# Attention in pairs of score tiles, with the weight conversion regrouped around it

## The chip, the cores and the metric

The kernel runs on one NeuronCore of a Trainium2 chip. Five engines have instruction queues of their own: TensorE (PE; its weight loads are shown apart as PEld), VectorE (DVE), ScalarE (ACT), GpSimd (POOL) and SyncE (SP), which here issues every DMA. The metric is the device time of one execution in microseconds (us).

## The reference

Two stages, in float32. Attention: batch 4, 8 heads, 576 positions, head width 64.

```
scores = q @ k.T / 8 + bias          # bias[h,i,j] = MLP(log1p|i-j| / log1p(max(i,1)))
attn   = softmax(scores); x = attn @ v
```

Then a mixer on x (4 x 576 x 512), with weights handed over as 64-bit floats:

```
u   = x + (x.T @ U @ V).T            # U 576x32, V 32x576
out = u + max(u @ w_ch1, 0) @ w_ch2  # 512 -> 2048 -> 512
```

## The kernel before, in words

**Order of the work.** The bias table of all heads is made first (about the first 60 us): a loop of 38 rounds, in each one score-bias block that PE multiplies, ACT copies out and SP stores to `bias_dram`. Then attention runs over 16 pairs of heads (batch 4 x 4 pairs), and then the mixer MLP. Nothing reorders the instructions: the schedule is manual, so each engine runs its instructions in the order in which the Python code emits them, and a waiting instruction holds all that stand behind it on its engine.

**A pair.** The 2 x 576 query rows of a pair are cut into 9 score tiles of 128 rows, s = 0 to 8 (tile 0 holds the last 64 rows of both heads). `slot(p, s)` (L489) emits the work of one tile:

- `scores` (L292): PE multiplies into a PSUM buffer `sc` (two of them, pool `psS`; tile 0 takes 8 matmuls, the others 4), and DVE adds the bias and takes the row extreme (L319). A buffer is free for the tile after next when DVE has read it.
- `exps` (L335): ACT takes the exponential in place (L338); for s = 0, 4, 8 it also sums up (L343).
- `tr`, `tr_m`, `tr_mid` (L378, L388, L397): PE transposes earlier tiles 128 x 128 at a time into one of three PSUM banks, and DVE or ACT copies them into `pt`. The first tile of a block is copied by DVE, the second by ACT; the last block of a pair is copied by ACT, and is transposed in slots 0 and 1 of the next pair.
- `av` (L411): the product of `pt` with v, in two halves of the query rows (half 0 is 320 columns wide, half 1 256). A half has five steps j. Steps 0 to 3 use 64-column weights, one per head, so that the two heads fill the two halves of the array; step 4 takes both heads in one 128-column matmul (L429). Each float32 matmul of these shows as two PE instructions. `AV_NEW` and `AV_OLD` say in which slot which steps stand: half 0 of a pair in its own slot 8 (j = 0, 1) and in slot 2 of the next pair (j = 2 to 4), half 1 in slots 4 (j = 0 to 2) and 6 (j = 3, 4) of the next pair. So a pair has four groups of products.
- `assemble` (L434): the product, copied by ACT to `ot`, is transposed again and scaled by DVE into `x_sb`.
- `recip` (L345): the reciprocal of the row sums on DVE, and for tile 0 a scaled copy `pm` on POOL (L358), which `tr_m` transposes in slot 5.

**Preparation of q and k.** `load_pair` brings the q and k of a pair into `raw` (one buffer), and `prep_ops` (L141) splits it on POOL into `hi` and `lo` by four instructions: `hi` (L153), its low part (L159), `hi`, `lo`. The scores of the next pair need all four. For pair 1 the raw data comes in three pieces (`second`, L692), of which the last, 16 KB, is issued in round 34 of the bias loop.

**Conversion.** The 64-bit weights are turned to float32 in jobs of 256 columns (`conv_ops`, L173): a load, then size and low (ACT, L185 and L188), clamp, shift, join (DVE, L191, L197, L203), add (POOL, L208), and a finish. `pipeline` (L618) cuts the jobs into three groups each, `[size, low, clamp]`, `[shift]`, `[join, add]`, and `background` emits the next groups behind the slots that `conv_at` names (six groups a pair). The first job is U (160 columns), three are V, whose finish `fin_v` is a copy on ACT and a subtraction on DVE (L611), and 16 are weights. Two empty groups stand behind the first loads.

**Mixer inside attention.** After each batch `mix_t` and five `mix_h` make u from x; they stand in pairs 5, 9 and 13 (`mix_t` ahead of slot 0) and, for the last batch, in the MLP.

Of the kernel before, what the change touches and what calls it, by code (L numbers as in the profile page):

```python
# [25 lines left out]
P = 128  # L26
# [11 lines left out]
AV_NEW = {8: (0, 1)}  # L38
AV_OLD = {2: [(0, 2), (0, 3), (0, 4)], 4: [(1, 0), (1, 1), (1, 2)], 6: [(1, 3), (1, 4)]}
# [5 lines left out]
def kernel(  # L45
# [365 lines left out]
    def av(p, hf, j):  # L411
        d = pair[p]
        pt = d["pt", hf]
        n = 320 if hf == 0 else 256
        v = v_t[p]
        if j == 0:
            d["o", hf] = psA.tile([P, 512], F32, tag="a", name="o")
        o = d["o", hf]
        if j < 4:
            for hd in range(2):  # L420
                mm(  # L421
                    o[hd * D : (hd + 1) * D, 0:n],
                    lhsT=v[:, (4 * hd + j) * D : (4 * hd + j + 1) * D],
                    rhs=pt[:, 5 * hd + j, :],
                    start=(j == 0),
                    stop=False,
                )
        else:
            mm(o[:, 0:n], lhsT=v[:, 8 * D : 8 * D + P], rhs=pt[:, 4, :], start=False, stop=True)  # L429
            ot = otp.tile([P, 320], F32, tag="ot", name="ot")  # L430
            copy("a", ot[:, 0:n], o[:, 0:n])
            d["ot", hf] = ot
# [56 lines left out]
    def slot(p, s):  # L489

        new, old = p < NP, p > 0
        if new:
            scores(p, s)
        if old and s == 0:
            tr(p - 1, 3, 0, "a")
        elif old and s == 1:
            tr(p - 1, 3, 1, "a")
            tr_mid(p - 1, 1, "d")
        elif old and s == 4:
            assemble(p - 1, 0)  # L500
# [11 lines left out]
        if s > 0 and new:
            recip(p, s - 1)
        elif s == 0 and old:
            recip(p - 1, 8)
        if old:
            for hf, j in AV_OLD.get(s, ()):
                av(p - 1, hf, j)
        if new:
            for j in AV_NEW.get(s, ()):  # L520
                av(p, 0, j)
# [96 lines left out]
    def pipeline(jobs):  # L618
# [5 lines left out]
        for i, (_, o, fin) in enumerate(ops):  # L624
# [3 lines left out]
            groups += [[size, low, clamp], [shift], [join, add]]  # L628
# [40 lines left out]
    for i in range(len(order) + 2):  # L669
# [18 lines left out]
        if i in (13, 17, 34):  # L688
# [7 lines left out]
    loads += [o for c in (4, 0, 1) for o in bias_loads(c, 1)] + [lambda: load_pair(2)]  # L696
    loads += [o for c in (2, 3) for o in bias_loads(c, 1)]
# [32 lines left out]
    for p in range(NP):  # L730
        if p > 0:
            new_pair(p)
        if 0 < p < HP - 1:
            bias[p + 1] = big.tile([P, 9 * S], F32, tag=f"big{p + 1}", name=f"bias{p + 1}")
            loads = [o for c in (4, 0, 1, 2, 3) for o in bias_loads(c, p + 1)]
        for s in range(9):
            if s == (1 if p else 0) and p < NP - 1:
                prep = prep_ops(p + 1)
            if s in ((2, 3, 4, 5) if p else (0, 1, 2, 3)) and p < NP - 1:
                prep.pop(0)()  # L740
            if s == 7 and 0 < p < NP - 2:
                load_pair(p + 2)
            if s == 7 and p + 1 < NP:
                load_v(p + 1)
            for o in loads[0:2]:
                o()
            del loads[0:2]
            if p > 0 or s not in early.values():
                if p > HP and p % HP == 1 and s == 0:
                    mix_t(p // HP - 1)  # L750
                slot(p, s)
                background(conv_at.get(s, 0))
            if p > HP and p % HP == 1:
                for c in {1: (4,), 2: (0,), 3: (1,), 4: (2,), 5: (3,)}.get(s, ()):
                    mix_h(p // HP - 1, c)
            if p == NP - 3 and s == 1:
                t = big.tile([P, 9 * S], F32R, tag="big0", name="w1q")
                *wq[0], uth[0] = big_views(t, [(WQ, KD), (WQ, KD), (LINE, None), (UT, KD)])
                feed = first_weights(0)
            if p == NP - 2 and s == 1:  # L760
                t = big.tile([P, 9 * S], F32R, tag="big1", name="w2q")
                w2a, w2b, utl[0] = big_views(t, [(WQ, KD), (WQ, KD), (LINE, None), (UT, KD)])
                wq[0] += [w2a, w2b]
                feed = first_weights(1)
            if p == NP - 1 and s == 1:
                t = big.tile([P, 9 * S], F32, tag="big2", name="acc")
                acc.update(enumerate(big_views(t, [(DM, 0)] * 10)))
                feed = iter(())
            if p >= NP - 3 and s in (1, 2, 4, 5, 7, 8):
                next(feed, None)  # L770
# [159 lines left out]
```

## Time and profile before

| | us |
|---|---|
| median of three runs | 786.69 (786.49 to 786.72) |
| the profiled execution | 785.47 |
| its span, first to last instruction | 783.7 |
| bias table | about 0 to 60 |
| attention, 16 pairs | about 32 to 360, the first four tiles inside the bias table |
| MLP | about 360 to 784 |

The rows shown below come from that one execution. A timeline row has the start, the length, engine, line, operation, tiles and count, and in brackets how long the engine stood idle before it and who released it. Runs of the same instruction are merged into one row, which then reaches from the first start to the last end. PE's matmuls overlap: how fast they follow each other is read from starts, not from lengths. [...]

### The profile page before, as it was taken

To read this page: it belongs to the slowest core of one execution; us is meant where nothing else is said; L and a number is where in the kernel's file an instruction comes from. 1 tells how busy PE (TensorE), PEld (TensorE's weight loads), DVE (VectorE), ACT (ScalarE), POOL (GpSimd) and SP (SyncE) were. 2 spreads that over 40 slices of the span, in tenths; PEclk is the share of its full clock that TensorE was granted. 3 is DMA by queue.
4 is the path that set the end of the run, shared out by engine and by line. 5 is a ranking of instruction groups with operands and counts; after the bars stand their busy time and mean duration, and the time that the engine had idled before them with its cause. 6 is when DMAs were issued, how large, how long until landed. Compare 5 with 4: busy or idle time off the path is not lost.

```text
span 783.7 us, 13761 instructions
## 1 busy us (share of the span) xinstructions
PE 753.5 (96%) x5292; PEld 617.6 (79%) x5292; DVE 420.3 (54%) x961; ACT 364.8 (47%) x819; POOL 232.1 (30%) x219
## 2 busy tenths in 40 slices
PE   6987699999999999999999999999999999999998
PEld 4435576677767777878789999899989999999886
DVE  7993476767666766664347834672237722221222
ACT  7994567767776776785115521441014401110010
POOL 0004555555555555660004611450005500000000
PEclk9998799999999999999999999999999999999999
DMA  7878984555655354750044300320003200001111
GB/s 226 253 264 254 272 235 111 148 160 130 151 144 174 94 117 102 214 166 1 1 165 131 107 23 15 94 95 14 1 1 95 81 1 1 1 28 54 55 41 68
DMA packets 39377, 84.01 MB, mean 107 GB/s; under 512 B 6800, under 2 KB 9488, under 8 KB 37264
## 3 DMA queue, kind: packets, MB, share of 16 engines
q1 hardware_dynamic: 39312, 83.13, 36.4%
q8 instruction: 42, 0.69, 0.4%
q14 instruction: 23, 0.19, 0.1%
HBM read 60.96 MB, written 22.15 MB: 106 GB/s over the span
## 4 chain that ended last, share of the span: by engine, by line
PE 81%; ACT 8%; DVE 4%; issue 3%; DMA 2%; POOL 1%; SPq 0%; DVEq 0%; ACTq 0%
PE ph L570 26%; PE po L593 25%; PE sc L317 7%; PE o L421 7%; PE tb L385 5%; ACT p L338 2%; PE o L429 2%; ACT ring L242 2%; PE bs L253 1%; DVE p L319 1%; PE mt L462 1%; ACT ring L264 1%; DMA wraw<-in_u_dram 1%; PE tu L543 1%; PE tm L393 1%
## 5 line engine op out<-in xcount | busy, mean ns | idle before, releaser
L575 ACT ACTIVATE hh<-ph 128x1024 fp32r<-128x1024 f32 x36 | 36.9, 1026 | 210.7 <-PE ph L570 210.7
L576 DVE SCALAR_TENSOR_TENSOR hh<-ph,hh 128x1024 fp32r<-128x1024 f32 x36 | 44.1, 1225 | 142.9 <-ACT hh L575 142.9
L319 DVE CUSTOM_DVE_ANT_0 p<-sc,bias 128x576 f32<-128x576 f32 x128 | 96.2, 753 | 42.7 <-PE sc L317 38.8
L317 PE MATMUL sc<-hi 128*128 128x288 f32 x320 | 105.4, 345 | 12.2 <-DVE st L319 12.2
L338 ACT ACTIVATE p<-p,st 128x576 f32<-128x576 f32 x128 | 99.8, 780 | 36.1 <-DVE st L319 35.8
L208 POOL TENSOR_TENSOR wy<-wt,wy 128x256 int32<-128x256 int32 (+1 forms) x68 | 50.1, 737 | 215.3 <-DVE wt L203 184.4
L593 PE MATMUL po<-wq,hh 128*128 128x512 f32 x432 | 103.2, 395 | 0.0
L593 PE MATMUL po<-w2q,hh 128*128 128x512 f32 x432 | 101.8, 391 | 0.0
L570 PE MATMUL ph<-ut,w1q 128*128 128x256 f32 x768 | 94.3, 280 | 0.0
L593 PEld LDWEIGHTS po<-wq,hh 128*128 128x128 f32 x432 | 80.1, 188 | 17.6
L570 PEld LDWEIGHTS ph<-ut,w1q 128*128 128x128 f32 x768 | 92.2, 188 | 1.9 <-issue 0.8
L317 PE MATMUL sc<-lo,hi 128*128 128x288 f32 x320 | 90.8, 299 | 2.1 <-POOL lo L159 2.1
L593 PEld LDWEIGHTS po<-w2q,hh 128*128 128x128 f32 x432 | 80.0, 188 | 16.1
L570 PEld LDWEIGHTS ph<-ut,wq 128*128 128x128 f32 x768 | 90.3, 188 | 1.4
L570 PE MATMUL ph<-ut,wq 128*128 128x256 f32 x768 | 90.6, 277 | 0.0
L596 DVE TENSOR_TENSOR acc<-po,acc 128x512 f32<-128x512 f32 x72 | 49.6, 690 | 72.8 <-PE po L593 72.8
L317 PEld LDWEIGHTS sc<-hi 128*128 128x128 f32 x320 | 61.2, 191 | 32.4 <-DVE st L319 13.1
L385 PE MATMUL tb<-ident,p 128*128 128x128 f32 x512 | 78.0, 275 | 0.8 <-DVE pt L367 0.5
L421 PE MATMUL o<-pt,v 128*64 128x256 f32 (+1 forms) x512 | 77.3, 423 | 0.0
L317 PEld LDWEIGHTS sc<-lo,hi 128*128 128x128 f32 x320 | 61.6, 193 | 4.2 <-POOL lo L159 2.4
L385 PEld LDWEIGHTS tb<-ident,p 128*128 128x128 f32 x512 | 62.1, 141 | 2.7 <-ACT p L338 1.2
L365 ACT COPY pt<-tb 128x512 f32<-128x512 f32 x88 | 50.9, 579 | 20.1 <-PE tb L385 19.5
(94 smaller groups left out, 1031.9 us busy)
## 6 DMA issues: line engine op xcount, KB each, us to landing
raw<-in_qk_dram SPq DMA_DIRECT2D x31, 608.0 KB, 7.6
wraw<-in_w_ch_dram SPq DMA_DIRECT2D x64, 256.0 KB, 2.7
bias_dram<-ring SPq DMA_DIRECT2D x36, 288.0 KB, 3.8
v<-in_vp_dram SPq DMA_DIRECT2D x16, 320.0 KB, 7.9
bias<-bias_dram SPq DMA_DIRECT2D x16, 288.0 KB, 4.8
acc<-u_dram SPq DMA_DIRECT2D x18, 256.0 KB, 4.8
out_dram<-acc SPq DMA_DIRECT2D x18, 256.0 KB, 2.0
bias<-bias_dram SPq DMA_DIRECT2D x16, 256.0 KB, 4.8
```

The lines of the kernel that those rows point to most:

```text
L208: nc.gpsimd.tensor_tensor(out=st["y"], in0=st["t"], in1=st["y"], op=ALU.add)
L317: mm(ps[:, a, 0:HALF], lhsT=hi[:, q0 : q0 + P], rhs=kk, start=(i == 0), stop=(i == n - 1))
L319: nc.vector.tensor_tensor_reduce(out=halves(dst), in0=ps[:, :, 0:HALF], in1=halves(bias[hp][:, s * S : (s + 1) * S]), scale=-0.125, scalar ...
L338: nc.scalar.activation(out=dst, in_=dst, func=AF.Exp, bias=st[:, s : s + 1], scale=-1.0, accum_out=st[:, 10 + s : 11 + s])
L365: nc.scalar.copy(out=out, in_=in_)
L385: nc.tensor.transpose(bank[:, kb, :], src[:, b0 + kb * P : b0 + (kb + 1) * P], ident)
L421: mm(o[hd * D : (hd + 1) * D, 0:n], lhsT=v[:, (4 * hd + j) * D : (4 * hd + j + 1) * D], rhs=pt[:, 5 * hd + j, :], start=(j == 0), stop=False,)
L570: mm(st["ps"][:, f, :], lhsT=w, rhs=u[:, k, :], start=(i == 0), stop=(i == 3 * KD - 1))
L575: nc.scalar.activation(out=hh[n], in_=st["ps"], func=AF.Relu)
L576: nc.vector.scalar_tensor_tensor(out=hl[n], in0=st["ps"], scalar=0.0, in1=hh[n].bitcast(F32), op0=ALU.max, op1=ALU.subtract)
L593: mm(ps, lhsT=h, rhs=w, start=(m == 0), stop=(m == 3 * FG - 1))
L596: nc.vector.tensor_tensor(out=a, in0=ps, in1=a, op=ALU.add)
```

## The change

Tiles are worked off two at a time (`slots`): scores and exponentials of both, then any product, then one conversion group, then the transposes and reciprocals of both, then a second conversion group. The first four tiles of pair 0 keep their places in the bias loop, so the couples are (4,5), (6,7), (8, 0 of the next pair), (1,2), (3,4), (5,6), (7,8) in odd pairs and (0,1), (2,3), (4,5), (6,7), (8, 0 of the next pair) in even ones. Products stand in two groups a pair, `AV_NEW` (half 0, in slot 8 of its own pair) and `AV_OLD` (half 1, slot 4 of the next), and step 4 is done per head with 64-column weights. A conversion job is cut into `[size, low]`, `[clamp, shift]`, `[join, add]`, five empty groups stand behind the first loads, and V's subtraction is on POOL. The last piece of pair 1's raw data is issued in round 32, and two sets of pair 1's bias loads are issued in rounds 28 and 30 instead of behind those of pair 0. `mix_t` stands between the scores of slots 1, 2 and their transposes.

```diff
-AV_NEW = {8: (0, 1)}
-AV_OLD = {2: [(0, 2), (0, 3), (0, 4)], 4: [(1, 0), (1, 1), (1, 2)], 6: [(1, 3), (1, 4)]}
+AV_NEW, AV_OLD = 8, 4
...
-    def av(p, hf, j):
+    def av(p, hf):
...
+        for j in range(5):
             for hd in range(2):
+                vb, pb = (4 * hd + j, 5 * hd + j) if j < 4 else (8 + hd, 4)
                 mm(
                     o[hd * D : (hd + 1) * D, 0:n],
-                    lhsT=v[:, (4 * hd + j) * D : (4 * hd + j + 1) * D],
-                    rhs=pt[:, 5 * hd + j, :],
+                    lhsT=v[:, vb * D : (vb + 1) * D],
+                    rhs=pt[:, pb, :],
                     start=(j == 0),
-                    stop=False,
+                    stop=(j == 4),
                 )
-        else:
-            mm(o[:, 0:n], lhsT=v[:, 8 * D : 8 * D + P], rhs=pt[:, 4, :], start=False, stop=True)
...
+    def slots(tiles, between):
+
+        for p, s in tiles:
+            scores(p, s)
+            exps(p, s)
+        between()
+        for p, s in tiles:
+            slot_av(p, s)
+        background(int(tiles[0][1] in conv_at))
+        for p, s in tiles:
+            slot_tr(p, s)
+            slot_recip(p, s)
...
-            nc.vector.tensor_tensor(out=v4l[:, a:e], in0=y, in1=v4h[:, a:e].bitcast(F32), op=ALU.subtract)
+            nc.gpsimd.tensor_tensor(out=v4l[:, a:e], in0=y, in1=v4h[:, a:e].bitcast(F32), op=ALU.subtract)
...
-            groups += [[size, low, clamp], [shift], [join, add]]
+            groups += [[size, low], [clamp, shift], [join, add]]
...
+        if i in (28, 30):
+            loads += bias_loads({28: 4, 30: 0}[i], 1)
...
-        if i in (13, 17, 34):
+        if i in (13, 17, 32):
             second.pop(0)()
...
-    queue[1:1] = [[]] * 2
+    queue[1:1] = [[]] * 5
...
-    conv_at = {0: 1, 1: 1, 6: 1, 7: 2, 8: 1}
+    conv_at = (0, 1, 2, 6, 7, 8)
...
+    for i in range(done, len(tiles), 2):
+        two = tiles[i : i + 2]
+        for t in two:
+            before(*t)
+        slots(two, lambda: [mix_t(p // HP - 1) for p, s in two if p > HP and p % HP == 1 and s == 1])
+        background(int(two[1][1] in conv_at))
+        for t in two:
+            behind(*t)
```

`before` holds what stood ahead of a slot (loads, `prep_ops`), `behind` what stood after it; `slot_tr`, `slot_recip` and `slot_av` are the parts of the old `slot`.

Where instructions move, in three places. First DVE at the end of pair 0 and the start of pair 1, before (`praw` is tile 0 of pair 1, `wt<-wt 128x160` the clamp of the U job; the bias tile's number 105 belongs to pair 0, 106 to pair 1):

```order
L319 ISA p,st<-sc,bias_105 128x576
L319 ISA st 128x1
L191 TENSOR_SCALAR wt<-wt 128x160
L319 ISA praw,st<-sc,bias_106 128x576
L319 ISA st 128x1
L350 RECIPROCAL st<-st 128x4
```

and now:

```order
L319 ISA p,st<-sc,bias_105 128x576
L319 ISA st 128x1
L319 ISA praw,st<-sc,bias_106 128x576
L319 ISA st 128x1
L350 RECIPROCAL st<-st 128x4
```

The clamp of the U job is gone from between the two tiles; it now stands behind tile 6 of pair 1, where both its clamp and its shift are issued:

```order
L319 ISA p,st<-sc,bias_106 128x576
L319 ISA st 128x1
L191 TENSOR_SCALAR wt<-wt 128x160
L197 TENSOR_SCALAR wt<-wt 128x160
L367 COPY pt<-tb 128x4x128
```

Second PE, the products of half 0 in an even pair's slot 2, before:

```order
L317 MATMUL sc<-hi 128x288
L317 MATMUL sc<-lo,hi 128x288
L421 MATMUL o<-pt,v 64x320 x4
L429 MATMUL o<-pt,v 128x320
L317 MATMUL sc<-hi 128x288
```

and now, behind tile 8 of a pair and tile 0 of the next:

```order
L317 MATMUL sc<-hi 128x288
L317 MATMUL sc<-lo,hi 128x288
L421 MATMUL o<-pt,v 64x320 x10
L439 MATMUL tx<-ident,ot 128x128 x2
L385 MATMUL tb<-ident,p 128x128 x8
```

All ten matmuls of the half stand together, with no 128-column one among them, and what follows is transposes. Third ACT in pair 7, from the exponential of tile 0 on, before:

```order
L338 ACTIVATE praw,st<-praw,st 128x576
L343 ACTIVATE st<-st,eps 128x1
L365 COPY pt<-tb 128x4x128
L338 ACTIVATE p,st<-p,st 128x576 x2
L365 COPY ot<-o 128x320
L338 ACTIVATE p,st<-p,st 128x576
```

and now:

```order
L338 ACTIVATE praw,st<-praw,st 128x576
L343 ACTIVATE st<-st,eps 128x1
L365 COPY ot<-o 128x320
L365 COPY pt<-tb 128x4x128 x2
L185 ACTIVATE wt<-wraw 128x256
L188 ACTIVATE wy<-wraw 128x256
L338 ACTIVATE p,st<-p,st 128x576 x2
L365 COPY pt<-tb 128x4x128
L338 ACTIVATE p,st<-p,st 128x576 x2
```

The copy that brings the last transposed tile of the pair before (`pt<-tb`, between the two rows of `x2`) stood ahead of the exponentials of tiles 1 and 2, and now stands behind both.

## Rows read from the trace of the kernel before

**Rows 1.** Windows by stage: stretch, length, busy (x instructions), granted clock, DMA share, GB/s.
```profile
72.00:84.70 12.70, 5.14 (x22) 4.70 (x22) 0.97 (x5) 1.07 (x4) 0.00 (x0) 0.50 1.00 273
...
102.00:255.00 153.00, 149.21 (x1028) 111.92 (x1027) 106.00 (x307) 110.89 (x283) 84.25 (x64) 1.00 0.58 155
255.00:344.00 89.00, 88.79 (x638) 69.03 (x637) 58.11 (x166) 66.94 (x166) 55.88 (x40) 1.00 0.50 127
...
360.00:784.00 424.00, 419.50 (x2728) 376.60 (x2724) 174.33 (x283) 99.03 (x204) 71.06 (x96) 1.00 0.15 50
```

**Rows 2.** Timeline 58 to 91 us, all engines, from pair 0 to pair 1.
```profile
58.90 0.50 SPq L125 DMA_DIRECT2D raw<-in_qk_dram  x1
...
63.71 1.21 POOL L153 TENSOR_SCALAR hi<-raw 128x1216 fp32r<-128x1216 f32 x1 [63.27 <-DMA raw<-in_qk_dram]
...
68.58 0.76 DVE L319 CUSTOM_DVE_ANT_0 p<-sc,bias 128x576 f32<-128x576 f32 x1 [3.46 <-DMA bias<-bias_dram]
...
72.00 0.61 PE L317 MATMUL sc<-lo,hi 128*128 128x288 f32 x1 [2.14 <-POOL lo L159]
...
83.35 0.34 ACT L185 ACTIVATE wt<-wraw 128x160 f32<-128x160 f32 x1 [11.50 <-DMA wraw<-in_u_dram]
...
83.72 0.24 DVE L191 TENSOR_SCALAR wt<-wt 128x160 f32<-128x160 f32 x1 [13.11 <-ACT wt L185]
...
83.88 0.75 DVE L319 CUSTOM_DVE_ANT_0 praw<-sc,bias 128x576 f32<-128x576 f32 x1
...
84.70 0.61 PE L317 MATMUL sc<-hi 128*128 128x288 f32 x1 [7.56 <-DVE st L319]
```

**Rows 3.** Windows from one `praw` reduction of DVE (L319) to the next.
```profile
102.62:121.96 19.34, 18.43 (x127) 13.41 (x125) 13.18 (x40) 13.70 (x38) 10.24 (x8) 1.00 0.84 232
121.96:140.55 18.59, 17.36 (x123) 13.19 (x122) 12.89 (x39) 13.51 (x37) 10.53 (x8) 1.00 0.43 108
181.01:198.18 17.17, 16.96 (x125) 13.31 (x124) 12.42 (x38) 13.31 (x36) 10.54 (x8) 1.00 0.49 121
198.18:215.43 17.25, 16.94 (x125) 13.28 (x124) 12.50 (x38) 13.33 (x36) 10.61 (x8) 1.00 0.54 140
255.61:271.79 16.18, 15.97 (x117) 12.32 (x116) 12.21 (x38) 12.36 (x32) 10.54 (x8) 1.00 0.28 71
271.79:288.39 16.60, 16.60 (x124) 13.19 (x123) 10.69 (x32) 12.28 (x33) 9.10 (x6) 1.00 0.46 109
```

**Rows 4.** Timeline of DVE 121 to 126 us, the finish of a V job.
```profile
124.17 0.29 DVE L611 TENSOR_TENSOR v4l<-wy,v4h 128x128 fp32r<-128x128 f32 x1 [1.18 <-ACT v4h L610]
```

**Rows 5.** Timeline of PE 255 to 264 us, groups of products between scores and transposes.
```profile
255.39 0.60 PE L385 MATMUL tb<-ident,p 128*128 128x128 f32 x4
...
256.78 0.30 PE L317 MATMUL sc<-hi 128*128 128x288 f32 x1
256.92 0.29 PE L317 MATMUL sc<-lo,hi 128*128 128x288 f32 x1
257.14 1.30 PE L421 MATMUL o<-pt,v 128*64 128x320 f32 x8
258.37 0.81 PE L429 MATMUL o<-pt,v 128*128 128x320 f32 x2
...
259.54 0.60 PE L385 MATMUL tb<-ident,p 128*128 128x128 f32 x4
...
261.37 1.52 PE L421 MATMUL o<-pt,v 128*64 128x256 f32 x12
```

**Rows 6.** Timeline of ACT 190 to 193 us, an exponential and a copy.
```profile
190.46 0.79 ACT L338 ACTIVATE p<-p,st 128x576 f32<-128x576 f32 x1
...
191.23 0.58 ACT L365 COPY pt<-tb 128x512 f32<-128x512 f32 x1
```

**Rows 7.** Timeline of POOL 183 to 196 us, `pm` and the last split of an even pair.
```profile
183.37 1.14 POOL L358 TENSOR_SCALAR pm<-praw,st 128x576 f32<-128x576 f32 x2 [3.96 <-DVE st L350]
...
190.64 2.79 POOL L159 TENSOR_TENSOR lo<-raw,hi 128x1216 fp32r<-128x1216 f32 x1
```

More of the change, by code (lines that the diff above doesn't have):

```diff
@@ L487, with slot_tr @@
     NP = B * HP
-    def slot(p, s):
+    def slot_tr(p, s):
         new, old = p < NP, p > 0
-        if new:
-            scores(p, s)
         if old and s == 0:
@@ L502, in slot @@
             assemble(p - 1, 1)
+        if new and s == 6:
+            tr_mid(p, 0, "d")
         if new and 3 <= s <= 8:
@@ L507, in slot, with slot_recip, slot_av @@
                 tr_m(p, "a")
-            elif s == 6:
-                tr_mid(p, 0, "d")
-        if new:
-            exps(p, s)
[L512 to L521, printed above, removed]
+    def slot_recip(p, s):
+        if s > 0 and p < NP:
+            recip(p, s - 1)
+        elif s == 0 and p > 0:
+            recip(p - 1, 8)
+    def slot_av(p, s):
+        if p > 0 and s == AV_OLD:
+            av(p - 1, 1)
+        if p < NP and s == AV_NEW:
+            av(p, 0)
+    def slot(p, s):
+        if p < NP:
+            scores(p, s)
+        slot_tr(p, s)
+        if p < NP:
+            exps(p, s)
+        slot_recip(p, s)
+        slot_av(p, s)
+    def slots(tiles, between):
+        for p, s in tiles:
+            scores(p, s)
+            exps(p, s)
+        between()
+        for p, s in tiles:
+            slot_av(p, s)
+        background(int(tiles[0][1] in conv_at))
+        for p, s in tiles:
+            slot_tr(p, s)
+            slot_recip(p, s)
     KD = DM // P
@@ L729, with before @@
     feed = iter(())
-    for p in range(NP):
-        if p > 0:
+    prep = []
+    def before(p, s):
+        nonlocal loads, prep
+        if s == 0 and p > 0:
             new_pair(p)
[L733 to L770, printed above, removed]
-            if p == NP - 1 and s in (1, 2, 3, 4, 5):
-                load_acc(2 * s - 2)
-                load_acc(2 * s - 1)
-            if p == NP - 1 and s in (6, 7):
-                make_ut(0, s - 6)
@@ new lines, in before @@
+            if p < HP - 1:
+                bias[p + 1] = big.tile([P, 9 * S], F32, tag=f"big{p + 1}", name=f"bias{p + 1}")
+                loads = [o for c in (4, 0, 1, 2, 3) for o in bias_loads(c, p + 1)]
+        if s == (1 if p else 0) and p < NP - 1:
+            prep = prep_ops(p + 1)
+        if s in ((2, 3, 4, 5) if p else (0, 1, 2, 3)) and p < NP - 1:
+            prep.pop(0)()
+        if s == 7 and 0 < p < NP - 2:
+            load_pair(p + 2)
+        if s == 7 and p + 1 < NP:
+            load_v(p + 1)
@@ new lines, in before, with behind @@
+        for o in loads[0:2]:
+            o()
+        del loads[0:2]
+    def behind(p, s):
+        nonlocal feed
+        if p > HP and p % HP == 1:
+            for c in {2: (4, 0, 1), 3: (2,), 4: (3,)}.get(s, ()):
+                mix_h(p // HP - 1, c)
+        if p == NP - 3 and s == 1:
+            t = big.tile([P, 9 * S], F32R, tag="big0", name="w1q")
+            *wq[0], uth[0] = big_views(t, [(WQ, KD), (WQ, KD), (LINE, None), (UT, KD)])
+            feed = first_weights(0)
+        if p == NP - 2 and s == 1:
+            t = big.tile([P, 9 * S], F32R, tag="big1", name="w2q")
+            w2a, w2b, utl[0] = big_views(t, [(WQ, KD), (WQ, KD), (LINE, None), (UT, KD)])
+            wq[0] += [w2a, w2b]
+            feed = first_weights(1)
+        if p == NP - 1 and s == 1:
+            t = big.tile([P, 9 * S], F32, tag="big2", name="acc")
+            acc.update(enumerate(big_views(t, [(DM, 0)] * 10)))
+            feed = iter(())
+        if p >= NP - 3 and s in (1, 2, 4, 5, 7, 8):
+            next(feed, None)
+        if p == NP - 1 and s in (1, 2, 3, 4, 5):
+            load_acc(2 * s - 2)
+            load_acc(2 * s - 1)
+        if p == NP - 1 and s in (6, 7):
+            make_ut(0, s - 6)
```

18 lines of the change are left out of this document (9 added, 9 removed).

## The prediction

> **What bounds the kernel now.** I read the windows by stage first, then the waits of each bad stage in the timeline, then the length of each pair. The windows [rows 1] show three regimes. From 360 us PE is busy for 419.5 of 424 us: the MLP is PE's own work, and the change touches it only by the conversion groups and the last products. From 102 to 344 us PE is busy nearly all the time, with DVE, ACT and POOL at about two thirds: attention is bound by what PE must stream, plus the gaps it is made to wait. [...]
>
> [...] PE waits until 72.00 for POOL's `lo` of pair 1; POOL began its four splits at 63.71, when the 16 KB raw piece issued at 58.90 had landed. Then PE does tile 0 and 1 of pair 1 and stops for 7.56 us until 84.70, for a score buffer that DVE has not read. DVE had nothing to do, yet its next instruction was the clamp of the U job, which waited 13.11 us for ACT's size, which waited 11.50 us for the DMA of U. The reduction of tile 0 stood behind the clamp and ran at 83.88, at once.
>
> A pair's own floor, from the spacing of starts [rows 5]: scores 40 x 0.134 = 5.4 us; transposes 46 x 0.108 = 5.0; products, two heads side by side, 10 steps x 0.269 = 2.7 for half 0 and 10 x 0.215 = 2.15 for half 1. Together 15.2 us. Each group of products adds a price for changing between 128- and 64-column weights: the last scores before one end at 256.92 + 0.13 = 257.05; the scores behind it end when the transposes start, 259.54, so began at 259.54 - 4 x 0.134 = 259.00; the group had 1.95 us for 6 x 0.269 = 1.61 us of streaming [rows 5]. That is 0.34 us a group, 1.36 for four. 15.2 + 1.36 = 16.6, which is the pair that has hardly any conversion (16.60), while pairs with conversion take 17.2, and those with V jobs about 19 [rows 3].
>
> **The change part by part.** All sums are against the profiled execution's 785.47 us.
>
> *Start of pair 1.* The U clamp moves from between tiles 8 and 0 to behind tile 6 of pair 1, some 15 us later; U landed at 83.35 [rows 2], and SP issues it behind much the same loads, so the clamp will find its data. The 7.56 us wait goes. The small raw piece goes out two rounds earlier but behind two bias loads; between 0 and 2.6 us (two rounds of 1.3), I take 1.6, so POOL ends its splits at about 70.4. What is late next: `lo` itself, since the reduction of tile 7 (bias landing, 68.58) ends at 69.3 [rows 2], before it. But PE now meets the scores of pair 1's tile 0 ahead of the products of half 0, which before filled part of the wait: PE stands idle from about 66 to 70.4. From there to the reduction of pair 2's tile 0 PE has to stream 48 score matmuls, 48 x 0.134 = 6.4 us, three groups of products (both halves of pair 0, half 0 of pair 1), 2.7 + 2.15 + 2.7 + 3 x 0.34 = 8.6, and 50 transposes, 5.4; with 0.2 of latency to DVE 20.6 us. [...] 70.4 + 20.6 + 1.75 + 2.75 = 95.5 against 102.62 [rows 3]: **-7 us**. [...] The five bias DMAs for pair 1 that move ahead run while the bias loop is bound by its engines, so I cost them at nothing; without that cover they delay the last bias rows, and tile 7, by up to 3 us.
>
> *Groups of products.* Four become two: 2 x 0.34 = 0.68 us a pair less streaming price, floor 15.9. Step 4 streams the same time: two passes of 0.269 either way (L429's two, or two side-by-side couples).
> [...]
>
> *New waits in the couples.* With the scores of two tiles in front, a copy on ACT stands behind two exponentials. Step on ACT: exponential to next instruction 0.77 (190.46 to 191.23), a copy 0.58 [rows 6]; a reduction on DVE 0.75 [rows 2].
> Odd pairs, couple (1,2), from the start of its scores: first reduction 0.73 to 1.4, exponentials 1.5 to 3.05, then the copy of the old pair's last block, ready at 3.65. PE has scores of four tiles 2.15 and transposes 0.65, so it is at `av` at 2.8: a wait of 0.85. Couple (5,6): the second exponential ends at 3.06, `tm` copies 0.54, the last copy ready at 4.2; PE arrives after 2.7 + 1.07 = 3.77: 0.45, and once more 0.45 in pairs 1, 5, 9, 13, where ACT does one copy more. Sum 1.3.
> Even pairs: the transpose in slot 3 needs the exponential of tile 1: about 0.25. The scores of the next pair's tile 0 now stand ahead of the half-0 products. POOL's `lo` ended 190.64 + 2.79 = 193.43, 10.1 us after `pm` began at 183.37 [rows 7], and `pm` will begin some 3.5 us into the pair: 13.6, while PE would be there at about 13. I take 0.55 for it, so 0.8 together (bounds 0 and 2.5).
> Mean 15.9 + 1.05 = 16.95.
>
> *Conversion.* DVE no longer waits for ACT inside a group, and V's subtraction, which held DVE 1.18 us [rows 4] ahead of a reduction, goes to POOL, which has 6 us to spare in a pair [rows 3]; without that slack it delays the splits by 0.75 each. So pairs 2, 3, 6, 7 go from 19.34 + 18.59 + 17.17 + 17.25 = 72.35 [rows 3] to 2 x (16.7 + 17.2) = 67.8: **-4.5** (bounds 0 and -9). Pairs 10 and 11, nearly free of waits, go from 32.78 [rows 3] to 33.9: **+1.1**. The three batches with `mix_t`, whose wait for `x_sb` at the top of slot 0 now has two score tiles in front of it, I give about -0.65 each, between the two kinds above: **-1.9**. Pairs 12, 14, 15: nothing. In the MLP two groups fewer: 2 x 0.34 = **-0.7**.
>
> Sum: -7 - 4.5 + 1.1 - 1.9 - 0.7 = -13.0, so 772.5 for the profiled execution. The median of the runs lies 1.22 above it: **773.7**, say 774.
>
> **The rivals.**
> *A, the stall only moves.* The start is fed by DMAs at a share of 1.00 and 273 GB/s [rows 1]. If the raw data of pair 2 or a bias tile lands late, `pm` of pair 1, now behind a split that needs that raw data, holds the transposes. For it: the full share. Against: the loads of pair 2's bias are not needed before 95 us. Gain at the start 2 instead of 7: 779.
>
> *B, slower.* The two-buffer scores and strict queues make every couple a closed loop: PE stops at `av` in both halves of each pair. Per group, two reductions 1.5, two exponentials 1.55, a copy 0.6, against 1.7 of PE's own work: 1.9 of wait, 3.8 a pair instead of my 1.05; where the transposes still cover half of that, 1.4 more than I take over 14 pairs, 774 + 20 = 794. It decides from 0.9 a pair (13 / 14) more than I take. For it: ACT is busy 13.3 of 17.2 us [rows 3], and a copy is late by exactly what stands ahead of it. Against: the products themselves, 2.5 to 3 us a group, let ACT catch up before the next couple. [...]
>
> [...]
>
> *D, better.* ACT runs ahead enough that half of the new waits don't show: 774 - 7 = 767; all of them, 759.
>
> **How the numbers follow.** The forecast, 768 to 781, has 0.60; A 0.13; B 0.09; C 0.03; D 0.15. What this kernel's measurement can tell from no change is about 0.2%, 1.6 us. Faster: all of the forecast, D and nearly all of A, two thirds of C, 0.88; same 0.04; slower 0.08, from B. The range goes from D's middle to where the forecast and A are out: 761 to 785.
>
> **What would show it.** Right: no DVE clamp that waits 13 us; the second `praw` reduction near 72 us and the third near 95; `praw` to `praw` of 16.7 to 17.2 us in pairs 2, 3, 6, 7; L429 gone and weight-load gaps at two groups a pair; PE waiting 0.5 to 1 us for ACT's `pt` copy ahead of L421 in odd pairs. Wrong: PE waiting on a DMA or on POOL for more than 3 us in pair 1; pairs above 18 us; or pairs 10 and 11 shorter than before, which would make my waits too high.

## The result: slower, 794.0 us, and the profile after

The changed kernel takes 793.99 us (median of five runs, 792.89 to 797.15) beside 786.72 for the kernel before on the same chip: a ratio of 1.0094, 95% interval 1.0070 to 1.0118. I had forecast 774, with 8 in 100 for slower. The profiled execution took 793.99 us, its span 792.1.

**Where the time went.** The windows of the changed kernel, from the reduction of one pair's tile 0 (`praw`) to that of a later pair (columns as in [rows 1], where the engines are PE, PEld, DVE, ACT and POOL, and the clock is the granted share of TensorE's full speed); the first row is pair 1, the next six are two pairs each, from 2 and 3 to 12 and 13, and the last is all that follows:

```profile
73.27:96.01 22.74, 21.40 (x153) 15.66 (x154) 10.13 (x32) 15.37 (x39) 9.41 (x7) 0.95 1.01 274
96.01:135.83 39.82, 35.30 (x255) 26.99 (x254) 27.41 (x75) 27.53 (x71) 22.93 (x21) 0.96 0.70 176
135.83:177.75 41.92, 38.86 (x279) 29.44 (x279) 27.81 (x78) 28.61 (x71) 21.11 (x17) 1.00 0.61 159
177.75:214.20 36.45, 33.57 (x254) 27.14 (x254) 27.67 (x75) 26.65 (x68) 21.48 (x17) 1.00 0.42 106
214.20:256.20 42.00, 38.92 (x279) 30.07 (x279) 27.53 (x79) 28.75 (x71) 21.47 (x17) 1.00 0.61 164
256.20:292.66 36.46, 33.61 (x254) 27.15 (x254) 27.10 (x72) 25.96 (x66) 21.04 (x16) 1.00 0.33 80
292.66:334.72 42.06, 38.44 (x279) 29.14 (x279) 24.28 (x66) 27.93 (x67) 20.62 (x14) 1.00 0.57 146
...
334.72:792.10 457.38, 450.70 (x2967) 401.47 (x2966) 197.85 (x343) 125.02 (x267) 88.34 (x110) 1.00 0.17 55
```

Pair 2 begins at 96.01 instead of 102.62 [rows 3]: -6.6 us. Pairs 2 to 13 then take 334.72 - 96.01 = 238.7 us; before it was 224.5 (to 327.09): +14.2. The rest takes 457.4 instead of 456.6: +0.8. That makes the +8.4 of the spans. Pairs 6 and 7, which I forecast at 33.9, take 36.45 (before 34.42 [rows 3]), and 10 and 11, also forecast at 33.9, 36.46 (before 32.78 [rows 3]). PE is idle for some 3 us of these 36.45, at a granted clock of 1.00.

**What PE waits for.** The waits of PE between 100 and 340 us in the changed kernel (who waits and for whom; sum in us, times, longest), the largest five:

```profile
PE tb L385 <- ACT pt L365: 7.5, 6, 1.4
PE sc L317 <- POOL lo L159: 3.4, 2, 2.5
PE tb L385 <- DVE pt L367: 2.2, 4, 1.0
PE sc L317 <- DVE st L319: 2.0, 2, 1.0
PE tm L393 <- DVE x_sb L367: 1.9, 2, 1.0
```

Before, the list had two rows. The first of them is still there, with 2.0 us instead of 2.9:

```profile
PE sc L317 <- DVE st L319: 2.9, 7, 0.8
PE tx L441 <- ACT ot L365: 0.8, 2, 0.4
```

The new waits are of transposes (`tb`, `tm`) for a PSUM bank that ACT or DVE has not copied out. The products (`o`), where I had looked for waits, have 0.4 us in this list. Here is the timeline of the changed kernel at three places (columns as in [rows 2]): the end of pair 0, pair 2, and the start of pair 6:

```profile
66.33 0.30 PE L317 MATMUL sc<-lo,hi 128*128 128x288 f32 x1
...
69.77 0.76 DVE L319 CUSTOM_DVE_ANT_0 p<-sc,bias 128x576 f32<-128x576 f32 x1 [4.82 <-DMA bias<-bias_dram]
...
70.68 0.58 PE L317 MATMUL sc<-hi 128*128 128x288 f32 x1 [4.05 <-DVE st L319]
...
73.16 4.06 PE L421 MATMUL o<-pt,v 128*64 128x320 f32 x20
...
102.67 1.21 POOL L153 TENSOR_SCALAR hi<-raw 128x1216 fp32r<-128x1216 f32 x1 [2.74 <-DMA raw<-in_qk_dram]
...
111.65 0.40 PE L317 MATMUL sc<-lo,hi 128*128 128x288 f32 x1 [2.46 <-POOL lo L159]
...
178.56 0.78 ACT L338 ACTIVATE praw<-praw,st 128x576 f32<-128x576 f32 x1 [1.39 <-DVE st L319]
...
179.66 0.76 ACT L338 ACTIVATE p<-p,st 128x576 f32<-128x576 f32 x1
...
180.00 0.29 PE L317 MATMUL sc<-lo,hi 128*128 128x288 f32 x1
...
180.42 0.42 ACT L185 ACTIVATE wt<-wraw 128x256 f32<-128x256 f32 x1
180.75 0.42 ACT L188 ACTIVATE wy<-wraw 128x256 int32<-128x256 uint32 x1
...
181.07 1.04 ACT L365 COPY pt<-tb 128x512 f32<-128x512 f32 x2
...
181.69 0.66 PE L385 MATMUL tb<-ident,p 128*128 128x128 f32 x4 [1.39 <-ACT pt L365]
...
182.64 2.79 POOL L159 TENSOR_TENSOR hi<-raw,hi 64x1216 fp32r<-64x1216 f32 x1
...
182.76 2.95 DVE L203 SCALAR_TENSOR_TENSOR wt<-wraw,sgn,wt 128x256 int32<-128x256 int32 x1
...
185.64 0.68 DVE L367 COPY pt<-tb 128x512 f32<-128x512 f32 x1
...
187.02 0.78 ACT L338 ACTIVATE p<-p,st 128x576 f32<-128x576 f32 x1 [3.19 <-DVE st L319]
...
188.34 0.63 PE L393 MATMUL tm<-ident,pm 128*128 128x128 f32 x4 [0.98 <-DVE x_sb L367]
```

At 70.68 PE has waited 4.05 us with both score buffers full, since DVE waited for the bias of tile 7 (the U clamp, which held DVE for 13 us [rows 2], is gone). The products of half 0 stand behind those scores and so can't fill the wait. In pair 2 POOL's splits wait 2.74 us for the raw data of pair 3 to land, and PE then 2.46 us for their `lo`; before, PE had no wait for `lo` after 100 us. At 180.13 PE reaches the transposes of step 3 and waits until 181.69 for the first of the bank copies that ACT begins at 181.07; ahead of the copy ACT has two exponentials, a sum, and size and low of the conversion. At 182.76 DVE begins a join that takes 2.95 us instead of 0.48 beside a split on POOL; the reductions, ACT's exponentials (3.19 us idle) and at 188.34 PE's transposes are late by it.

### The profile page after: what moved, and what is told of

Read it like the earlier page. It is cut to its first block, busy times and chain, and to the rows that moved or that the text cites. A ratio compares the mean times of both kernels' runs of the same rounds, so it can differ in the third digit from the quotient of the medians.

```text
span 792.1 us, 13854 instructions
## 1 busy us (share of the span) xinstructions
PE 749.1 (95%) x5356; PEld 618.1 (78%) x5356; DVE 430.0 (54%) x958; ACT 366.6 (46%) x819; POOL 234.6 (30%) x222
## 4 chain that ended last, share of the span: by engine, by line
PE 66%; DMA 9%; POOL 9%; ACT 8%; DVE 4%; issue 3%; SPq 1%; POOLq 0%; DVEq 0%; ACTq 0%
PE po L612 25%; PE ph L589 25%; PE o L421 6%; DMA raw<-in_qk_dram 4%; PE sc L317 4%; ACT ring L242 3%; POOL lo L159 2%; POOL hi L159 2%; PE tb L385 2%; POOL hi L153 2%; ACT p L338 2%; DMA bias<-bias_dram 1%; DVE p L319 1%; DMA bias_dram<-ring 1%; ACT ring L264 1%
## 5 line engine op out<-in xcount | busy, mean ns | idle before, releaser
L319 DVE CUSTOM_DVE_ANT_0 p<-sc,bias 128x576 f32<-128x576 f32 x128 | 92.3, 752 | 30.3 <-PE sc L317 25.0
L317 PE MATMUL sc<-hi 128*128 128x288 f32 x320 | 95.2, 319 | 6.2 <-DVE st L319 6.1
L421 PE MATMUL o<-pt,v 128*64 128x320 f32 (+1 forms) x640 | 91.6, 422 | 0.7 <-ACT pt L365 0.4
L317 PE MATMUL sc<-lo,hi 128*128 128x288 f32 x320 | 88.7, 298 | 3.7 <-POOL lo L159 3.6
L385 PE MATMUL tb<-ident,p 128*128 128x128 f32 x512 | 73.7, 276 | 12.2 <-ACT pt L365 8.8
L385 PEld LDWEIGHTS tb<-ident,p 128*128 128x128 f32 x512 | 57.7, 141 | 25.7 <-ACT pt L365 10.5
L421 PEld LDWEIGHTS o<-pt,v 128*64 128x64 f32 x640 | 48.3, 140 | 33.1 <-issue 7.8
L153 POOL TENSOR_SCALAR hi<-raw 128x1216 fp32r<-128x1216 f32 x30 | 36.6, 1220 | 110.6 <-DMA raw<-in_qk_dram 86.2
```

Source lines behind the costliest of these rows:

```text
L153: nc.gpsimd.tensor_scalar(out=hi[:, a:e], in0=raw[:, a:e], scalar1=1.0, scalar2=0.0, op0=ALU.mult, op1=ALU.add)
L317: mm(ps[:, a, 0:HALF], lhsT=hi[:, q0 : q0 + P], rhs=kk, start=(i == 0), stop=(i == n - 1))
L319: nc.vector.tensor_tensor_reduce(out=halves(dst), in0=ps[:, :, 0:HALF], in1=halves(bias[hp][:, s * S : (s + 1) * S]), scale=-0.125, scalar ...
L385: nc.tensor.transpose(bank[:, kb, :], src[:, b0 + kb * P : b0 + (kb + 1) * P], ident)
L421: mm(o[hd * D : (hd + 1) * D, 0:n], lhsT=v[:, vb * D : (vb + 1) * D], rhs=pt[:, pb, :], start=(j == 0), stop=(j == 4),)
```

## The experiments

Eighteen kernels. Each ratio is to the kernel before, run between them on the same chip (median 786.0 to 786.4).

**The halves of the change.** *e1*: the kernel before with the conversion groups, five empty groups, v4l on POOL and the early loads; no more.

> This is the kernel before with the first half of the change alone: the conversion regrouped (clamp and shift together, five empty groups ahead, v4l on POOL) and the loads of pair 1 asked for earlier. Score tiles go one at a time and the products stand in their old places. Theory W (the loss sits in the order by two tiles, where transposes wait for PSUM banks whose copy stands behind two exponentials on ACT): the start is worth its 6.6 us at pair 2 (the first tile of pair 2 is reduced at 96 instead of 102.6 us), and the pairs after it are as long as before, so 778 to 781 us. Theory P (the loss sits in the input chain, DMA of raw, splits on POOL, next raw, which the regrouped conversion and the earlier start have made tight, with pm and v4l on POOL): the pairs 2 to 13 get longer here too, by most of the 14 us that they lost in the changed kernel, so 786 to 792 us.

773.5 us, 0.9844 [0.9822, 0.9866]: faster by 12 to 13 us, more than theory W had. In its profile (776.74, the slowest of its five runs, 8.7 us below the one before) pair 2 begins at 94.33 and pairs 2 to 13 take 223.6 us, 0.9 less than before. Theory P falls: the pairs don't get longer by these edits.

*e2*: the kernel before with the products of a half together.

```diff
-AV_NEW = {8: (0, 1)}
-AV_OLD = {2: [...], 4: [...], 6: [...]}
+AV_NEW, AV_OLD = 8, 4
```

> This is the kernel before with one thing changed: the products of one half stand together (at steps 4 and 8) instead of in four places. Theory W: the price of a change between groups on PE (0.34 us each, two such places saved in a pair) is real and nothing in single-tile order takes it back, so -0.3 to -0.7 us in each of 16 pairs, 776 to 782 us. Theory P says the same of this kernel. Rival G (a long group of products is itself what hurts, since the next scores and the bank copies wait behind 2.5 us of products): 786 to 792 us.

786.61 us, 1.0007 [0.9992, 1.0021]: no gain, at the edge of Rival G's band, though not by its mechanism. From the starts of PE's matmuls in pairs 3 to 14: the gaps at the edges of products (those next to the mixing left out) fall from 15.5 to 7.2 us, 0.69 a pair, as priced. But the gaps between scores and transposes rise from 0.4 to 8.5. PE's waits for ACT's exponential, not there before, show it (waits of PE, 100 to 340 us, e2):

```profile
PE tb L384 <- ACT p L337: 6.1, 9, 0.8
PE sc L316 <- DVE st L318: 4.2, 5, 1.9
```

The product pieces in step 2 had covered the exponential that step 3 needs. *e3*, both:

> Both of the above in one: the regrouped conversion, the earlier loads and the products in two groups, with score tiles one at a time. It is the changed kernel without its order by two tiles. Theory W: the two savings add, 769 to 775 us. Theory P: the input chain takes them back, 784 to 792 us. Whatever it takes, its distance to the changed kernel (794) is what the order by two tiles costs with everything else equal: by W some 20 us, by P under 8.

774.37 us, 0.9853 [0.9832, 0.9874], in W's band. But the grouping adds nothing here either. The changed kernel is e3 plus the order by two tiles, and plus the place of the mixing that went with it: the five `mix_h` of a batch stand behind tiles 1 to 5 in e3 as before, one each, and in the changed kernel three of them stand in a row.

```diff
-                for c in {1: (4,), 2: (0,), 3: (1,), 4: (2,), 5: (3,)}.get(s, ()):
+            for c in {2: (4, 0, 1), 3: (2,), 4: (3,)}.get(s, ()):
```

Together they cost 793.99 - 774.37 = **19.6 us**. Plain pairs, which have no mixing, show it too. Pairs 6 and 7, then 8 and 9, which have one, in e3:

```profile
170.07:203.82 33.75, 32.76 (x254) 26.25 (x253) 24.84 (x74) 26.38 (x68) 21.13 (x16) 1.00 0.47 124
...
203.82:242.47 38.65, 38.16 (x279) 29.54 (x278) 27.95 (x79) 28.23 (x72) 21.09 (x16) 1.00 0.62 169
```

The changed kernel takes 36.45 and 42.00 for them.

**The order inside a couple.** *e4*, *e5* and *e6* move the parts of `slots`, *e7* three copies from ACT to DVE; in short:

```text
 e4: scores(both) av(both) tr(both) exps(both)
 e5: scores(both) exps(first) av(both) tr(first) exps(second) tr(second)
 e6: scores(first) tr(first) scores(second), ACT: exps(both) then copies; tr(second) av(both)
 e7: -tr(p - 1, 3, 0, "a")  -tr(p - 1, 3, 1, "a")  -tr_m(p, "a")
     +tr(p - 1, 3, 0, "d")  +tr(p - 1, 3, 1, "d")  +tr_m(p, "d")
```

> This is the changed kernel, still by two tiles, with the order of ACT's and DVE's work inside a couple turned round: the transposes and their copies out of PSUM are issued ahead of the couple's two exponentials, and both groups of the conversion behind them; PE's order stays. Theory W: the banks come free two exponentials earlier (about 1.4 us), and the waits of transposes for banks (14 us of PE's idle time at the transitions from scores and from ti to tb, 3 from o to tb) mostly go; the exponentials end later, of which a part is waited for in the next couple: 778 to 787 us. Theory P, or that the waits are for the joins slowed on DVE by POOL: 791 to 796 us.

807.18 us, 1.0267 [1.0247, 1.0287]: slower than either theory had. The banks come free, and now the exponentials are late (waits of PE, e4):

```profile
PE tb L385 <- ACT p L338: 10.1, 17, 1.4
PE sc L317 <- DVE st L319: 6.2, 8, 1.1
```

> The changed kernel with ACT's order inside a couple interleaved: exponential of the first tile, copies of the first tile's blocks, exponential of the second tile, copies of the second tile's blocks. PE's order stays by two tiles (both scores, products, transposes). With both exponentials first (the changed kernel) PE waits 7.5 us for copies (120 to 330 us of the trace); with both copies first it waits 9.4 us for exponentials. Theory W (ACT's order inside the couple is the cost, either end of it is late): each wait is halved or better, 778 to 786 us. Rival V (PE's own order is the cost: transposes of two tiles back to back after scores and products back to back need more than three banks at once, whatever ACT does): 791 to 797 us.

794.89 us, 1.0091 [1.0064, 1.0119]: as Rival V had it. At the same place as 181.69 above PE waits the same 1.39 us, now for ACT's exponential. Since all three orders of the same ACT work leave a wait there, ACT's order alone isn't the cause.

> The other half of that question: PE goes by one tile again (scores, transposes, scores, transposes, products at the end), while ACT keeps the changed kernel's order (both exponentials, then the copies). Theory W: still slow, 788 to 798 us. Rival V: PE's order was the cost, so back near the 774 us of the kernel with both savings and single tiles, 774 to 780 us.

819.95 us, 1.0414 [1.0383, 1.0445]: outside both. Holding ACT's copies behind two exponentials hurts a PE that goes by one tile even more (11.9 us of `tb` waiting for ACT's copies, 16.0 of `sc` for DVE).

> The changed kernel with three bank copies a pair (both blocks of tr(p-1,3,.) and the two small ones of tr_m) on DVE instead of ACT, so that no block of a couple at a pair's start stands behind exponentials. Theory W: the longest waits (1.4 us at the first transposes of slot 3, once in two pairs, and those of tb and tm behind them) go, DVE has room (67% busy), 782 to 789 us. If DVE's two reductions delay the copies as ACT's exponentials did, or the cost is spread over all transitions: 791 to 797 us.

797.78 us, 1.0134 [1.0104, 1.0163]: a miss for W, and a little above the other band. The waits for ACT's copies fall to 2.7 us, and `sc` waits 6.1 instead of 2.0 for DVE.

PE's clock has a part in e5, e6 and e7. In their traces the granted clock is 0.5 for 3.4 to 6.8 us at a time, two, three and three times in pairs 4 to 13 (the mean from 113 to 335 us is 0.98, 0.96 and 0.97); in the changed kernel it is 1.00 in these pairs. What sets such a stretch off was not shown. The two executions of e7 with a mean granted clock of 0.994 and 0.996 took 793.9 and 794.4 us, as the changed kernel does, and the four with 0.987 to 0.989 took 797.1 to 800.0. The two of e5 with 0.993 and 0.995 took 791.0 and 790.9. So at a like clock e7 costs nothing more than the changed kernel, and e5 some 3 us less.

**Cover, place and start.** *e8* is e3 with `AV_OLD = 2`; *e9* is the changed kernel with before's four places of products.

> The kernel with both savings and single tiles (774.4), its second group of products moved from step 4 to step 2. With the products in two groups PE has nothing but scores and a few transposes in steps 0 to 3, comes to the first transposes of step 3 before ACT has written their exponential, and waits 0.63 us there and 0.35 in the scores ahead of it, which is what the fewer group edges had saved. Theory C (the scattered products were the cover of ACT's exponentials): the group between scores 2 and 3 covers them, -0.3 to -0.9 us in each of 15 pairs, 762 to 770 us; if the group then waits for the copies of the last block, half of it. If the waits come from something else: 773 to 776 us.

776.75 us, 0.9870 [0.9849, 0.9891]: no gain over e3. The wait for the exponential goes (0.4 us left of 6.3 in e3), so products in step 2 do cover it, but now the products wait 2.5 us for ACT's copies and transposes 2.6 for DVE.

> The changed kernel, by two tiles, with the products in the four places of the kernel before (steps 2, 4, 6 of the next pair and 8 of its own) instead of two groups. Theory C (the products were PE's cover for exponentials and copies, and the couples need that cover most): a product piece stands in nearly every couple, the 1.6 us wait at step 3 of every even pair and the 0.6 us waits behind couples without products shrink, the group edges come back (0.5 us a pair), 784 to 790 us. Theory O (the order by two tiles costs by itself, wherever the products stand): 792 to 800 us.

788.6 us, 1.0026 [1.0010, 1.0041]: 5.4 us less than the changed kernel, in C's band. The waits of `tb` for ACT's copies fall from 7.5 to 1.6 us. But by two tiles it is still 15.1 us slower than e1, its twin by single tiles.

*e10*: `conv_at = (3, 4, 5, 6, 7, 8)` in the changed kernel.

> The changed kernel with its six conversion groups of a pair in steps 3 to 8 instead of 0, 1, 2, 6, 7, 8. At a pair's start ACT has two exponentials, a sum, two bank copies and size and low (0.75 us) for a couple in which PE has scores and transposes only; the transposes of step 3 wait 1.6 us for it in every even pair. Theory A (ACT is the bound there, by its work and not by its order, since both other orders of that work left the wait at 1.6): the wait falls by the 0.75 us, 7 times, and DVE's joins move away from POOL's splits or beside other ones, 785 to 791 us. If the waits only move to the couples that now carry the conversion: 792 to 796 us.

804.64 us, 1.0239 [1.0215, 1.0262]: the wrong way, so theory A isn't tested by it. Here is why, in the timeline of e10 in pair 6:

```profile
190.76 1.21 POOL L153 TENSOR_SCALAR hi<-raw 128x1216 fp32r<-128x1216 f32 x1
...
190.91 1.21 DVE L191 TENSOR_SCALAR wt<-wt 128x256 f32<-128x256 f32 x1
...
192.06 2.76 POOL L159 TENSOR_TENSOR lo<-raw,hi 128x1216 fp32r<-128x1216 f32 x1
192.15 2.81 DVE L197 TENSOR_SCALAR wt<-wt 128x256 int32<-128x256 int32 x1
...
194.88 0.75 DVE L319 CUSTOM_DVE_ANT_0 p<-sc,bias 128x576 f32<-128x576 f32 x1
...
195.69 0.40 PE L317 MATMUL sc<-hi 128*128 128x288 f32 x1 [2.69 <-DVE st L319]
```

Clamp and shift take 0.29 us each in the changed kernel (the median). Here the clamp takes 1.21 and the shift 2.81: each begins within a POOL split (0.15 and 0.09 us behind its start) and ends after it (by 0.15 and 0.14), and the reduction behind them, and then PE, wait. Summed between 60 and 370 us, what the clamps, shifts and joins of 256 columns took above their median is some 24 us in e10, 9 in the changed kernel, 6 in e1 and 1 before.

*e11*: the tiles of pair 0 and the first of pair 1 one at a time. *e12*: groups `[size, low], [clamp, shift, join], [add]`.

> The changed kernel with the tiles of pair 0 that stand in the attention loop, and the first of pair 1, one at a time; couples from the second tile of pair 1 on. In the changed kernel PE waits 4.1 us at 66.6 us, since the scores of the couple (0,8), (1,0) stand ahead of the 2.9 us of products and both score buffers are held until the bias of tile (0,7) has landed at 69.8; with single tiles the products ran in that wait. Theory S (4.6 of the 20 us between the order by one and by two are lost in this place): -3 to -5 us, 789 to 791 us. If the input of pair 1 or 2 decides what follows, or it is given back in pair 1: 793 to 796 us.

795.37 us, 1.0120 [1.0101, 1.0140]: no gain. Pair 2 begins at 94.11, 1.9 earlier, and pairs 2 to 5 take 83.8 instead of 81.7: PE waits there 1.1 us for a copy of DVE ahead of `tm` and 0.8 for POOL's `hi`, which it does not in the changed kernel.

> The changed kernel with the join of the conversion in the group of clamp and shift, ahead of POOL's splits, its POOL add staying in the third group. In the changed kernel two joins took 2.95 us instead of 0.48 while POOL's L159 ran, and the transposes of tm waited for the DVE copy behind them. Theory X (DVE slowed beside POOL is a good part of the loss): 2 to 4 us less than the changed kernel, 789 to 792 us. Otherwise within 1.5 us of it.

797.9 us, 1.0145 [1.0120, 1.0169]: slower than either had; theory X isn't borne out. The longest join shortens from 2.95 to 1.3 us, but `sc` waits 6.9 us for DVE, and PE's granted clock is 0.5 three times in pairs 4 to 13 (the one execution with a mean of 0.992 took 794.2 us, the five with 0.986 to 0.988 took 796.7 to 800.5).

**What is left when the guests go.** The guests are the conversion and the mixing, which are no part of attention itself. *e13* and *e14* take the conversion's work out of the changed kernel and of e3, *e15* and *e16* POOL's low splits, *e17* and *e18* conversion and mixing.

```text
 e13, e14: +return load, [none] * 5 + [lambda: finish(bias[0][:, 0:n])], none
 e15, e16: -lambda: low(hi[D:P, 0:K0], 0, K0, D)  -lambda: low(lo, K0, QKW, 0)   `lo` is the high half of k
 e17, e18: mix_t: +if b < B - 1: return      mix_h: +the store only
```

> The changed kernel without the work of the conversion of the first weights in attention (ACT's size and low, DVE's clamp, shift and join, POOL's add are left out of those 16 jobs; their loads and stores stay, the stores from other data). To be set against the same with single tiles. Theory R (the order's own resources cost the 20 us): 785 to 792 us, and 12 us or more above its single-tile twin. Theory K (the conversion's work on ACT, and its DVE operations slowed beside POOL's splits, is what the couples can't bear): 772 to 779 us, at most 8 above its twin.

> The kernel with both savings and single tiles (774.4) without the same work. ACT's lateness at step 3 (0.63 + 0.34 us a pair) loses the 0.75 us of size and low where they stand in steps 0 to 2: 763 to 771 us by either theory; it is the reference for its two-tile twin.

786.85 (1.0021 [1.0004, 1.0038]) and 774.19 us (0.9855 [0.9836, 0.9875]): 12.7 us apart instead of 19.6. e13 is inside R's band, e14 is no faster than e3, against both. The windows of pairs 6 and 7, then 8 and 9, of e13:

```profile
174.29:208.38 34.09, 32.86 (x254) 26.16 (x254) 21.22 (x62) 24.24 (x60) 18.11 (x12) 1.00 0.41 107
208.38:250.76 42.38, 38.43 (x279) 29.14 (x279) 24.25 (x66) 26.07 (x63) 18.11 (x12) 1.00 0.63 173
```

and of e14:

```profile
170.23:203.94 33.71, 32.19 (x254) 26.14 (x253) 21.34 (x62) 23.91 (x60) 18.11 (x12) 1.00 0.50 132
203.94:242.30 38.36, 37.61 (x279) 29.39 (x278) 24.07 (x66) 25.80 (x63) 18.14 (x12) 1.00 0.60 164
```

Without the conversion plain pairs cost nearly the same by two tiles as by one (34.09 and 33.71), where with it they cost 2.7 us more; pairs with a mixing cost 4.0 us more. Whether that is the order or the three `mix_h` in a row, no run tells.

> The changed kernel without POOL's two low splits for the pairs 1 to 15 (the low halves of q and k are left out, and the products that used them take the high halves, so PE's work is the same); raw is then free 5.5 us earlier and the long POOL instructions beside DVE are gone. Theory K's other half, I (the input chain and DVE slowed beside POOL): 778 to 784 us, at most 10 above its single-tile twin. Theory R: 787 to 793 us, and 14 or more above its twin.

> The kernel with both savings and single tiles (774.4) without the same two splits: its waits for POOL are 1 to 3 us in all, at pairs 1 and 2, so 769 to 774 us by either theory; it is the reference for its two-tile twin.

788.05 (1.0034 [1.0020, 1.0048]) and 769.68 us (0.9797 [0.9778, 0.9815]): 18.4 apart. Both kernels gain, 6 and 5 us, the difference stays: POOL's low splits are not what makes the couples dear. Theory R's numbers hold here.

> The changed kernel without the conversion's work (as before) and without the mixing of batches 0 to 2 (mt, th, tl, mh and their sums are left out, the stores of x_sb stay). Theory M (what the couples can't bear are the guests, conversion on ACT and DVE and the mixing's extra banks, and the order itself is about free): 768 to 772 us, at most 4 above its single-tile twin. Theory R (the order itself costs): 775 us or more, 8 or more above its twin.

> The kernel with both savings and single tiles, without the same two: three batches' mixing is some 2.7 us of products and edges on PE each, so 764 to 768 us; it is the reference for its two-tile twin.

774.65 (0.9853 [0.9825, 0.9881], runs from 771.8 to 777.9) and 764.87 us (0.9726 [0.9707, 0.9744]): 9.8 apart. That is past M's bound of 4 and R's of 8 is met, with a time just below R's 775. With both guests gone PE still waits for banks, for POOL's `lo` and, once for 4.3 us at the end of pair 0, for a score buffer (waits of PE, 60 to 340 us, e17):

```profile
PE tb L388 <- ACT pt L368: 7.2, 7, 1.8
PE sc L320 <- POOL lo L159: 6.7, 6, 1.8
PE sc L320 <- DVE st L322: 5.3, 2, 4.3
```

So by the medians the 19.6 us divide like this, each taken from a pair of twins: 6.9 with the conversion's work, 2.9 with the mixing, 9.8 that stay with the order itself. From the 95% intervals I estimate that the difference of two twins is known to some 2.5 us, so the 2.9 is not told from nothing. The 5.4 us of e9 were measured across this division and are not a fourth part of it.

By place the traces divide it otherwise (spans, two tiles less one, us; one execution each):

| twins | in all | up to the start of pair 4 | pairs 4 to 13 | behind them |
|---|---|---|---|---|
| changed kernel and e3 | 19.5 | 4.1 | 15.7 | -0.3 |
| e13 and e14, no conversion | 12.5 | 1.1 | 11.5 | -0.2 |
| e17 and e18, nor mixing | 8.0 | 0.1 | 4.7 | 3.1 |

In pairs 4 to 13, where most of the loss is, 4.2 us go with the conversion, 6.8 with the mixing and its place, and 4.7 stay with the order itself. The 3.1 us behind pair 13 show in e17 alone.

## Why the prediction was wrong

By place: the start was forecast at -7 and came at -6.6; pairs 2 to 13 at -5.3 (-4.5, +1.1 and -1.9) and came at +14.2; what follows at -0.7 and came at +0.8.

- *Start of pair 1*, -7: right, -6.6, in both of its `praw` times (73.27 and 96.01 for some 72 and 95.5). PE's idle stretch came where I put it, though its end was set by the bias of tile 7 as well as by POOL. Of the sum's last two terms, 1.75 is the waits of an odd pair (1.3, and 0.45 once more in pair 1), and 2.75 is a loss at half clock, an assumption of mine that no run shows. What the changed kernel shows is a granted clock of 0.50 from 68.7 to 75.5 us, with score matmuls 0.24 us apart (71.59 to 72.79) that are 0.13 apart at 1.00 (66.06 to 66.33), and PE busy for 4.82 us of that stretch, so a loss of some 2.4 (an estimate, half of the busy time). Of the 8.7 us that e1's profile gains, 8.3 are this step. In the changed kernel 2.5 of the 6.6 us are given back in pair 2, where the raw data of pair 3 lands too late (102.67 and 111.65 in the timeline).
- *Groups of products*, 0.68 us a pair: the size is right (0.69 in e2), the gain is nil. The step failed where it subtracted the edges from the pair's floor and left the rest of the pair as it was. Cutting two groups of products out of steps 2 and 6 removed the work behind which ACT made the exponentials; PE came sooner and waited (0.4 to 8.5 us between scores and transposes). I never asked what those pieces covered.
- *New waits in the couples*, 1.05 us a pair: **the step that turned the sign.** Plain pairs came out at 18.2 instead of 16.95, 1.3 a pair more than I took, and at 16.9 by single tiles (e3). I followed the products' wait for their last copy, and where I did the size was fair: the products of the couple that I gave 0.85 take 3.10 us at 200.08, 0.7 more than at 183.63, though pairs 5, 9 and 13 don't show it. I did not follow the transposes, which need one of three banks each, nor the conversion's size and low, which stand on ACT ahead of the copies, nor DVE's instructions beside POOL. Without the conversion's work plain pairs take 17.05 by two tiles (e13), so in them it is this work among the couples that makes most of the difference.
- *Mixing*, -1.9 in pairs 4, 5, 8, 9, 12 and 13: these came out at 41.92 + 42.00 + 42.06 = 126.0 us instead of 119.3 before, +6.6. I looked at one wait, that of `mix_t` for `x_sb`, and priced nothing for the `mix_h` that now stand three in a row and take banks from the same three as the transposes. In pairs 8 and 9 two tiles cost 4.0 us more than one also without the conversion (e13, e14), and 2.0 with the mixing gone too (e17 36.8, e18 34.8).
- *Conversion*, -4.5 in pairs 2, 3, 6 and 7: right in two of the four pairs. In e1, where it stands with single tiles and the old products, pairs 6 and 7 take 33.19, the floor of 2 x 16.6 that I worked from. Pairs 2 and 3 take 38.34 instead of 37.93 [rows 3]: PE waits 2.4 us there for POOL's `lo`, whose first split waited 4.9 for the raw data of pair 3. I also did not count that clamp, shift and join now stand beside POOL's splits.
- *Rivals.* B came true in sign and price (794), and its bound of 0.9 us a pair was passed; that the price fits so well is luck, since PE stops at the transposes, for banks and exponentials, and not at `av`. A had the right kind of late data, but it fell on pair 3 and cost 2.5 us. That the grouping gains nothing (786.61 us in e2) is not because the edges are free: with half as many groups the gaps there fall by 0.69 us a pair.

Not settled: which resource makes up what stays with the order itself (9.8 us by the medians, 4.7 in pairs 4 to 13 by the traces), and how much of the mixing's part is the place of `mix_h`. Waits for banks, for score buffers and for POOL's `lo` all show in e17, and every kernel that freed one of them (e4, e5, e7, e11) met the next. A fourth bank, a third score buffer or the old place of `mix_h` in the changed kernel, which would tell them apart, wasn't tried.

The best kernel measured that does all of the work is e1, 773.5 us, with e3 (774.4) within the noise; it has the regrouped conversion and the early loads alone and beats both the kernel before and the changed one.

## What to carry to other kernels

Before a gap on the bound engine is counted as saved, look at what the engines that feed it are doing in that gap: here the pieces of products that cost 0.69 us of edges a pair hid just as much of ACT's work. When a change has parts that can stand alone, price them one by one and also together, since here one gained 12 us and another lost 20. Where instructions are regrouped, list what then runs beside what on engines off the critical path, too.

## What the hardware did that I had not expected

Conversion instructions of DVE that started within a POOL split ended only behind it. Between 60 and 370 us there are seven in the kernel before (clamps) and nine in the changed one (clamps, shifts and joins), and they end 0.07 to 0.28 us after the split: the join at 182.76 takes 2.95 us instead of 0.48. The shift of e10 takes 2.81 instead of 0.29. The reductions took 0.74 to 0.76 us in all 144 cases of both kernels, also in the 42 and 55 that started within a split between 60 and 370 us. When DVE was first by 0.01 to 0.09 us, five times in the changed kernel, its clamp, shift or join kept its 0.29 or 0.48 us and POOL's split took longer, 1.26 to 1.35 us instead of 1.21 (L153) or 3.04 instead of 2.79 (L159), as the timeline in pair 8 shows:

```profile
219.21 0.48 DVE L203 SCALAR_TENSOR_TENSOR wt<-wraw,sgn,wt 128x256 int32<-128x256 int32 x1
219.30 3.04 POOL L159 TENSOR_TENSOR hi<-raw,hi 64x1216 fp32r<-64x1216 f32 x1
```

Here the join starts 0.09 us ahead of the split, keeps its 0.48 us, and the split takes 3.04 instead of 2.79. The starts alone don't tell which one waits: at 122.40 us in e10 a join that starts 0.04 ahead of the split takes 2.96 us. Why the two wait for each other was not shown.
